# Splitting an early input transfer, moving a small one to another queue, and setting products further from the transfers that feed them, in a one-core attention and feed-forward kernel

## The chip, the core and the metric

The kernel runs on one core of one Trainium2 chip. The metric is the device time of one execution in microseconds (us). Each kernel was executed five or six times in a set of runs, beside the kernel before on the same chip. A profile belongs to one of those executions; its span is 1.73 us shorter than the device time of the same execution (155.57 less 153.84 before).

## The reference, cut to what matters

```python
# x: 2048 tokens x 448; wqkv 448 x 1344; w_phi 16 x 28 x 28; wo 448 x 448; w1 448 x 1792; w2 1792 x 448; bf16
xn = layernorm(x)
q, k, v = heads(xn @ wqkv)                       # 16 heads of 28
phi(t) = concat(softmax(t @ w_phi), softmax(-(t @ w_phi)))
o = (phi(q) @ (phi(k).T @ v)) / (phi(q) @ sum(phi(k)) + 1e-6)     # linear attention
out = x + o @ wo + silu(xn @ w1) @ w2
```

## The kernel before

The kernel has a list of operations with dependencies, and a greedy scheduler that orders them per engine when the program is built, from modelled durations. `chain` adds order alone. `cur_slack` makes the scheduler place a product that much later than the modelled end of what it waits for; it is not a wait on the chip.

The loads are issued in this order (SP queue unless `eng` says otherwise):

```python
load(Wp[:], A_w_phi.rearrange("(g hl) d f -> (hl d) g f", g=G), "wphi", eng="act", lat=3000.0)
load_x(0, 1)
load_x(1, 2)
load_x(2, 4)                     # token tiles 2 and 3 in one transfer
load_w1(0, 512, 3200.0)          # two transfers each: 384 rows, and the last 128
load_w1(512, 1024, 3200.0)
load_x(4, 8)
load_w1(1024, FF)
# ... wv, x tiles 8 to 15, w2, wo
```

`w_phi` is 448 pieces of 56 bytes. The layernorm of tiles 0 to 3 goes through DVE and ACT, and PE transposes them; tiles 4 to 15 go through DVE and POOL, and a transposing DMA takes two tiles at a time:

```python
def ln_tile(t):                  # cut
    # bn_stats, bn_aggr (DVE); sqrt on ACT and reciprocal, or pow on POOL; (x - mean) * rstd (DVE)
    if t >= XN_DMA0:             # 4
        if t % 2:
            dma_t(xnT[:, t - 1:t + 1, :, :]..., xn_sb[:, sl - 1:sl + 1, :]..., 1300.0, f"xnT_dma{t}")
        return
    transposes(...)              # tiles 0 to 3, on PE
```

At the start PE computes 38 products of ones that nobody reads, to bring its clock up. Then come the transposes of tiles 0 and 1, then ffn1 (w1) for tiles 0 to 3. The next products that need new tokens are those of ffn1 for tiles 4 to 7, which I call the second quarter:

```python
for i in range(38):
    P.op("pe", 107.0, ... banks[3][:, 0:128], ones_bf[:], ones_bf[:] ..., name="warm")
# ...
for t in range(4):
    ln_tile(t)
fold()                           # block diagonal of w_phi, one POOL operation
chain("ev0 ve2 ev1 ve3 ev2 silu_table".split())
# ... ffn1 of tiles 0 to 3: F(0) to F(6); v of tiles 0, 1
for n, t in ((7, 2), (10, 4)):   # F(7) is the first product that needs tiles 4 to 7
    group([F(n, 0), v_block(t, AUX)], [F(n + 1, 2), F(n + 2, 4)], "rem")
```

The output stage multiplies by wo what a transposing DMA delivers:

```python
def wo_fulls(q, ob, cs, st):
    P.cur_slack = 900.0
    for n in range(3):
        mm(ob, oT_sb[:, q, n + q % 2, :], wo_sb[:, q % 2, n, cs], st and n == 0, False, "wo_mm")
    P.cur_slack = 0.0
```

The softmax here doesn't subtract the row's maximum and nothing guards it: scores larger than these inputs give would overflow.

## Time and profile before

| | us |
|---|---|
| median of the first three executions | 153.57 (153.53 to 153.88) |
| the profiled execution | 155.57, span 153.84 |
| PE busy | 148.2 |

From the page of the kernel before: the span, PE's busy time with its number of instructions, then PE's busy tenths and the granted PE clock in tenths, in 40 equal slices of the span.

```profile
span 153.8 us, 2800 instructions
...
PE 148.2 (96%) x1118; PEld 79.4 (52%) x1118; DVE 90.0 (59%) x171; ACT 72.6 (47%) x86; POOL 67.4 (44%) x76
...
PE   7599999999999999999999999999999999999993
...
PEclk9959999999999999999999999999999999999999
```

PE is the limit; only the head is loose, and the clock was down in the third slice. From the table of waits of the kernel before, PE alone (us in total, times, longest):

```profile
PE psum L438 <- DMA phT<-in_B_w_dram: 1.3, 1, 1.3
PE psum L490 <- POOL ones_bf L465: 1.1, 1, 1.1
PE psum L453 <- DVE rstd L569: 0.4, 1, 0.4
PE psum L438 <- DMA vaug<-vaug: 0.2, 1, 0.2
```

`phT<-in_B_w_dram` is w1 (it borrows that tile's room), and `vaug<-vaug` is a transposing DMA ahead of wo.

The stretches of the head (bounds and length, then for PE, PE's weight loads, DVE, ACT and POOL the busy time and count, then clock, DMA share, GB/s), for the kernel before:

```profile
4.00:6.00 2.00, 1.56 (x21) 1.19 (x18) 1.56 (x6) 0.86 (x3) 0.30 (x1) 1.00 0.93 302
6.00:7.45 1.45, 0.12 (x3) 0.03 (x1) 1.12 (x3) 0.60 (x3) 0.00 (x0) 1.00 1.05 356
7.45:9.40 1.95, 1.95 (x22) 1.95 (x23) 1.29 (x6) 0.75 (x3) 0.00 (x0) 0.58 1.04 382
9.40:10.90 1.50, 1.50 (x17) 1.50 (x16) 0.00 (x0) 1.04 (x2) 0.00 (x0) 0.50 1.06 390
```

### The profile page before, as it was taken

How to read it: one execution, taken by the hardware profiler on the slowest of the kernel's cores; microseconds unless marked ns; L12 is line 12 of the kernel's file. 1: busy time of each engine (PE TensorE's matmuls, PEld its weight loads, DVE VectorE, ACT ScalarE, POOL GpSimd, SP SyncE). 2: the span in 40 equal slices, each digit the busy share in tenths (PEclk: the TensorE clock that was granted, in tenths of full speed). 3: DMA queues.
4: the chain of work that ended last, by engine and by line, in shares of the span. 5: the costliest groups of instructions: out<-in, count | busy, mean ns of one | idle time of the engine just before them, and what ended most of it. 6: DMA issues, size and time to landing. Idle time of an engine off the chain costs nothing.

```text
span 153.8 us, 2800 instructions
## 1 busy us (share of the span) xinstructions
PE 148.2 (96%) x1118; PEld 79.4 (52%) x1118; DVE 90.0 (59%) x171; ACT 72.6 (47%) x86; POOL 67.4 (44%) x76
## 2 busy tenths in 40 slices
PE   7599999999999999999999999999999999999993
PEld 7497444446444556545434444445554455555482
DVE  1748888306019998897112521999973724474552
ACT  3452884676688669698555759784000000000000
POOL 7105564300014999999993000499997000000000
PEclk9959999999999999999999999999999999999999
DMA  5997554799940000000058311065899993144151
GB/s 90 320 387 285 112 105 81 91 240 280 238 137 0 4 0 0 9 0 0 4 114 161 66 34 38 0 122 98 171 124 191 207 199 68 39 124 124 36 155 64
DMA packets 44206, 17.38 MB, mean 113 GB/s; under 512 B 36640, under 2 KB 43808, under 8 KB 44192
## 3 DMA queue, kind: packets, MB, share of 16 engines
q1 hardware_dynamic: 41568, 15.44, 45.3%
q10 hardware_dynamic: 2624, 1.75, 3.8%
q8 instruction: 9, 0.15, 0.4%
q14 instruction: 5, 0.04, 0.1%
HBM read 6.56 MB, written 1.84 MB: 55 GB/s over the span
## 4 chain that ended last, share of the span: by engine, by line
PE 91%; DMA 6%; SPq 1%; issue 0%; DVE 0%
PE psum L438 90%; DMA phT<-in_B_w_dram 3%; DMA vaug<-vaug 3%; SPq L499 1%; PE psum L453 1%; DVE x_sb L776 0%
## 5 line engine op out<-in xcount | busy, mean ns | idle before, releaser
L438 PE MATMUL psum<-xnT,phT 128*128 128x512 bf16 (+2 forms) x278 | 49.2, 346 | 1.3 <-DMA phT<-in_B_w_dram 1.3
L438 PE MATMUL psum<-w_sb,hT 128*128 128x448 bf16 (+1 forms) x238 | 48.6, 342 | 0.0
L458 ACT ACTIVATE hT<-psum 128x1024 bf16<-128x1024 f32 x28 | 27.9, 1025 | 18.8 <-PE psum L438 18.8
L706 POOL TENSOR_TENSOR RA<-Ek_sb,Rec 128x896 bf16<-128x896 bf16 x16 | 26.6, 1700 | 16.3 <-DVE Rec L674 16.3
L438 PEld LDWEIGHTS psum<-xnT,phT 128*128 128x128 bf16 (+1 forms) x278 | 21.1, 102 | 21.6 <-issue 4.7
L438 PEld LDWEIGHTS psum<-w_sb,hT 128*128 128x128 bf16 x238 | 22.2, 98 | 17.4 <-issue 0.6
L673 DVE TENSOR_REDUCE Rec<-Ek_sb 128x64 f32<-128x1792 bf16 x12 | 23.7, 1978 | 12.0 <-ACT Ek_sb L458 12.0
L458 ACT ACTIVATE Ek_sb<-psum 128x896 bf16<-128x896 f32 x24 | 20.4, 927 | 5.0 <-PE psum L438 2.3
L681 POOL TENSOR_TENSOR Ek_sb<-Ek_sb,Rec 128x896 bf16<-128x896 bf16 x8 | 13.3, 1698 | 5.7 <-DVE Rec L674 5.6
L753 DVE TENSOR_SCALAR den<-psum 128x16 f32<-128x16 f32 x16 | 2.7, 171 | 19.6 <-PE psum L438 19.6
L438 PE MATMUL psum<-wv,xnT 128*128 128x448 bf16 (+1 forms) x64 | 13.5, 352 | 0.0
L438 PE MATMUL psum<-Wk,xnT 128*128 128x448 bf16 (+1 forms) x64 | 13.5, 353 | 0.0
L681 POOL TENSOR_TENSOR phT<-phT,Rec 128x896 bf16<-128x896 bf16 x8 | 13.3, 1706 | 0.0
L438 PE MATMUL psum<-Wq,xnT 128*128 128x448 bf16 (+1 forms) x64 | 12.5, 353 | 0.0
L438 PE MATMUL psum<-wo_sb,vaug 128*128 128x448 bf16 (+1 forms) x51 | 11.7, 342 | 0.2 <-DMA vaug<-vaug 0.2
L563 DVE BATCH_NORM_STATS2 st<-x_sb 128x6 f32<-128x448 bf16 x16 | 9.6, 602 | 3.7 <-DMA x_sb<-in_A_x_dram 3.7
L776 DVE TENSOR_TENSOR x_sb<-psum,x_sb 128x448 bf16<-128x448 f32 (+1 forms) x13 | 7.1, 583 | 5.9 <-PE psum L438 5.8
L760 DVE TENSOR_TENSOR vaug<-psum,rden 128x448 bf16<-128x448 f32 x16 | 10.0, 624 | 0.8 <-DVE rden L755 0.2
L578 DVE TENSOR_SCALAR RA<-x_sb,mv,rstd 128x384 bf16<-128x384 bf16 (+2 forms) x28 | 8.8, 350 | 2.7 <-POOL rstd L574 2.6
L674 DVE RECIPROCAL Rec<-Rec 128x64 f32<-128x64 f32 x16 | 8.7, 546 | 0.3
L673 DVE TENSOR_REDUCE Rec<-phT 128x64 f32<-128x1792 bf16 x4 | 8.0, 1990 | 0.9 <-ACT phT L458 0.9
L572 POOL TENSOR_SCALAR ve<-mv 128x1 f32<-128x1 f32 x12 | 2.6, 217 | 13.2 <-DVE mv L564 13.2
(49 smaller groups left out, 118.2 us busy)
## 6 DMA issues: line engine op xcount, KB each, us to landing
out_dram<-x_sb ACTq DMA_DIRECT2D x15, 112.0 KB, 2.6
w_sb<-in_B_w_dram SPq DMA_DIRECT2D x1, 1568.0 KB, 8.0
x_sb<-in_A_x_dram SPq DMA_DIRECT2D x3, 448.0 KB, 7.4
phT<-in_B_w_dram SPq DMA_DIRECT2D x2, 384.0 KB, 5.3
wo_sb<-in_A_wo_dram SPq DMA_DIRECT2D x2, 336.0 KB, 4.0
phT<-in_B_w_dram SPq DMA_DIRECT2D x1, 576.0 KB, 7.1
wv<-in_A_wqkv_dram SPq DMA_DIRECT2D x1, 336.0 KB, 7.2
phT<-in_B_w_dram SPq DMA_DIRECT2D x2, 128.0 KB, 5.2
```

The source lines that it names most:

```text
L438: r = e.matmul(dst, lhsT, rhs, start=st, stop=sp, skip_group_check=True)
L458: P.op("act", d_act(n), lambda e: e.activation(dst, src, func, scale=scale), reads=[src], writes=[dst], table=table, name=name, **keys)
L563: P.op("dve", 590, lambda e: e.bn_stats(st6[:, t, :], xs), reads=[xs], writes=[st6[:, t, :]], name=f"bnst{t}", okeys_w=["ln"])
L572: P.op("pool", 200, lambda e: e.tensor_scalar(ve[:, t:t + 1], mv[:, t, 1:2], EPS_LN, None, ALU.add), reads=[mv[:, t, 1:2]], writes=[ve[:, ...
L578: P.op("dve", dur, lambda e: e.tensor_scalar(dst, x_sb[:, t, c0:c1], mv[:, t, 0:1], rstd[:, t:t + 1], ALU.subtract, ALU.mult), reads=[xs, ...
L673: P.op("dve", 1985, lambda e: e.tensor_reduce(R2, E4, AXL.X, ALU.add), reads=[E4], writes=[R2], name="Ssum")
L674: P.op("dve", 555, lambda e: e.reciprocal(R2, R2), reads=[R2], writes=[R2], name="Rrec")
L681: P.op("pool", 1700, lambda e: e.tensor_tensor(E3, E3, Rk[:, :, None].broadcast_to([128, 32, DH]), ALU.mult), reads=[E3, Rk], writes=[E3], ...
L706: P.op("pool", 1700, lambda e: e.tensor_tensor(dst, Eq, Rq.rearrange("p (c j) -> p c j", c=CC)[:, :, :, None].broadcast_to([128, CC, 4, DH ...
L753: P.op("dve", 190, lambda e: e.tensor_scalar(den[:, uq, :], U3[:, :, DH], EPS_DEN, None, ALU.add), reads=[U3[:, :, DH]], writes=[den[:, uq ...
L760: P.op("dve", 620, lambda e: e.tensor_tensor(o3, U3[:, :, 0:DH], rden[:, uq, :, None].broadcast_to([128, H, DH]), ALU.mult), reads=[U3[:, ...
L776: P.op("dve", d_dve(cs.stop - cs.start), lambda e: e.tensor_tensor(res[:, cs], ob, addend[:, cs], ALU.add), reads=[ob, addend[:, cs]], wri ...
```

## The change

Its intent: let the first tiles and w1 come sooner, by taking w_phi's small pieces out of the head and letting tile 2 arrive without tile 3; and take away the last wait of a wo product.

```diff
-        load(Wp[:], A_w_phi.rearrange("(g hl) d f -> (hl d) g f", g=G), "wphi", eng="act", lat=3000.0)
         load_x(0, 1)
         load_x(1, 2)
-        load_x(2, 4)
+        load_x(2, 3)
+        load_x(3, 4)
         load_w1(0, 512, 3200.0)
@@ wo_fulls, and the same in finish_tile
-            P.cur_slack = 900.0
+            P.cur_slack = 1500.0
@@
-        fold()
         act(warm_act[:], ones_bf[:, 0:4], ACTF.Silu, 4, "silu_table", table="silu", okeys_w=["sq"])
-        chain("ev0 ve2 ev1 ve3 ev2 silu_table".split())
+        load(Wp[:], A_w_phi.rearrange("(g hl) d f -> (hl d) g f", g=G), "wphi", eng="act", lat=3000.0)
+        chain("ev0 ve2 ev1 ve3 ev2 silu_table wphi".split())
@@ after the layernorm of tiles 4 to 7
         chain("ev3 bnst4".split())
+        fold()
+        chain("rstd7 bdphi".split())
```

w_phi was on the scalar queue already; it is now issued there later. The order of operations on PE changes only around the transposes of tiles 2 and 3 and around the wo products.

More of the change, by code (lines that the diff above doesn't have):

```diff
@@ L790, in finish_tile @@
                 wo_fulls(q, ob, cs, t < NYT)
-                P.cur_slack = 900.0
+                P.cur_slack = 1500.0
                 pe_mms([wo_rem(q, ob, slice(0, 128), cs)], "wo_mm")
```

## The prediction

> **What bounds it.** The matrix engine (PE): busy 148.2 of 153.8 us (first table), 91% of the chain of waits. Its waits (table of waits): 1.3 us for w1's first transfer, 1.1 us for the ones tile at the start, 0.4 us for the first layernorm, 0.2 us for one transposing DMA before a wo product at 123.2 us. Only the head, that gap and the PE clock can give anything. The table of stretches shows clock 0.58 from 7.45 to 9.40 us and 0.50 to 10.90 us; 128-column matmuls start 107 ns apart there, 56 ns later. [...] (half from 7.76 to 11.17 us). It costs 1.7 us.
>
> **The head in the trace.** x tiles 0 and 1 land at 3.1 and 3.5 us, tiles 2 and 3 (one transfer) at 6.27, w1's first block at 7.32, issued at 2.20. Between 2.9 and 5.4 us most of the 16 DMA engines hold one packet of tiles 2 and 3 for 0.4 to 1.4 us; others of that size take 74 ns. They come just behind w_phi's 448 packets of 56 B. [...] I take the stall to be w_phi's, unproved.
>
> **What the change does.**
> - Takes w_phi out of the head. If the stall goes, w1's first block lands near 5.7 us (estimate: issue 0.45 us later, first packet 1.1 us after issue, 24 packets per engine at 47 ns, 0.4 us to land). Then the copy of transposed tile 0 gates PE (ends at 6.33 us): PE starts near 6.4, not 7.45 us: 1.0 us.
> - ACT's second copy, queued behind a square root of tile 2, ends near 7.3, not 7.96 us.
> - One more issue on the SP queue: w1 and later loads are issued 0.45 us later, the loss if the stall stays.
> - w_phi's issue (0.42 us on ACT) falls in a 2.8 us hole; its product (0.93 us on POOL) in a 1.48 us hole after rstd 7. Free.
> - wo products move behind more ffn2 matmuls of 0.19 us: removes the 0.2 us wait, adds no work (1118 matmuls as before).
>
> **Clock.** With PE back at 6.4 us, the window from 4.35 to 7.76 us holds about twice the matmul work. If that keeps the clock full, 1.7 us more come, less what later loads take back.
>
> **Sum.** Stall gone, half-clock stays: 1.0 + 0.2, 152.4 us (35%). Stall and half-clock gone: 2.2 + 0.2, 151.2 us (25%). Stall stays: 0 to 0.3, 153.4 us (40%). Predicted **152.4 us**, 151.0 to 153.7 us 8 times in 10. Faster by over 2% 0.07, within 2% 0.92, slower 0.01.
>
> **What shows it.** Right: PE's wait for w1 under 0.5 us; no 1 us packets in tiles 2 and 3; w1's first block lands before 6.3 us; no wait at 123 us; PE busy the same, or 1.5 us less if the clock row has no 5. Wrong: w1 lands at 7.3 us or later.
>
> **What would make it wrong.** The slow packets come from something else; the stall moves with w_phi to 12 us and delays x tiles 4 to 7 or w1's last block; a late w_phi blocks POOL and the layernorm of tiles 8 and 9.

The sum: 1.0 (PE's start) and 0.2 us (the wo wait) off 153.6 us, 152.4 us. So was the paragraph on the clock, behind the 151.2 us branch: in the trace of before PE was busy for 1.66 us from 4.34 to 7.76 us and the clock was 0.50 in the next 3.41 us, but that the second follows from the first is not shown. The estimate of 5.7 us is from the same trace: one issue on the SP queue takes 0.45 us, tile 0's first packet started 1.04 us after its issue, w1's 1 KB packets took 46 ns in the median and 49 in the mean, and w_phi landed 0.44 us after its last packet. Its terms, counted from w1's issue at 2.20 us, come to 5.3 us.

## More of the kernel before

From the timeline of the kernel before (start, duration, engine, line, operation, count, and in brackets the idle time before it with what ended it):

```profile
6.30 0.63 DVE L563 BATCH_NORM_STATS2 st<-x_sb 128x6 f32<-128x448 bf16 x1 [0.63 <-DMA x_sb<-in_A_x_dram]
...
7.45 1.93 PE L438 MATMUL psum<-xnT,phT 128*128 128x128 bf16 x19 [1.33 <-DMA phT<-in_B_w_dram]
...
11.25 0.62 DVE L563 BATCH_NORM_STATS2 st<-x_sb 128x6 f32<-128x448 bf16 x1
...
20.68 2.75 PE L438 MATMUL psum<-xnT,phT 128*128 128x512 bf16 x12
```

The first line is tile 2's statistics, the second the first ffn1 products, the third tile 4's statistics, which wait for nothing here. The last is six products of tiles 0 to 3 and then the first six of the second quarter, without a pause.

## The result, and the profile after

| | before | after |
|---|---|---|
| median of five executions, us | 153.56 (153.33 to 153.88) | 153.48 (153.14 to 153.89) |
| ratio | | 0.9993, 95% interval 0.997 to 1.0016 |
| profiled execution, us | 155.57 | 153.50 |
| span, us | 153.84 | 151.77 |

Ratios here and below are the mean time of one kernel's fast runs over that of the other's of the same rounds, so they are not quite the ratio of the medians quoted. By the 2% rule of the verdicts every run below is "the same" as the kernel before; what is said of smaller differences rests on the intervals and on the traces.

The medians say: the same. The two profiles differ by 2.07 us. Both are true, because the profile of before belongs to an execution that took 2.0 us more than that kernel's median. From the page after, the lines shown of before:

```profile
span 151.8 us, 2800 instructions
...
PE 147.0 (97%) x1118; PEld 78.3 (52%) x1118; DVE 90.5 (60%) x171; ACT 72.5 (48%) x86; POOL 67.4 (44%) x76
...
PE   7799999999999999999999999999999999999993
...
PEclk9999999999999999999999999999999999999999
```

PE's waits in the kernel after, whole:

```profile
PE psum L490 <- POOL ones_bf L465: 1.1, 1, 1.1
PE psum L438 <- ACT xnT L458: 0.9, 1, 0.9
```

The second line is again the wait for w1: the first transfer of its first block landed at 6.98 us and the product began at 7.11, while the copy of transposed tile 0 had ended at 6.38 us; the profile names what it saw last. The timeline after:

```profile
5.43 0.62 DVE L563 BATCH_NORM_STATS2 st<-x_sb 128x6 f32<-128x448 bf16 x1
...
7.11 1.22 PE L438 MATMUL psum<-xnT,phT 128*128 128x128 bf16 x19 [0.93 <-ACT xnT L458]
...
10.94 0.63 DVE L563 BATCH_NORM_STATS2 st<-x_sb 128x6 f32<-128x448 bf16 x1 [1.42 <-DMA x_sb<-in_A_x_dram]
...
18.72 2.94 PE L438 MATMUL psum<-xnT,phT 128*128 128x512 bf16 x12
```

Three things are to be seen. Tile 2's statistics start 0.87 us sooner, as intended. The first 19 products take 1.22 us where they took 1.93: the clock. And tile 4's statistics, which used to wait for nothing, now wait 1.42 us for x tiles 4 to 7; the twelve products across the border to the second quarter take 2.94 us where they took 2.75, so PE waited 0.2 us inside them. The stretches after:

```profile
4.00:6.00 2.00, 2.00 (x21) 1.71 (x18) 1.89 (x7) 0.72 (x3) 0.00 (x0) 1.00 0.83 234
6.00:7.45 1.45, 0.52 (x9) 0.37 (x8) 1.34 (x7) 1.33 (x4) 0.00 (x0) 1.00 1.08 364
7.45:9.40 1.95, 1.95 (x38) 1.95 (x36) 0.80 (x4) 0.79 (x2) 0.00 (x0) 1.00 1.00 335
9.40:10.90 1.50, 1.50 (x30) 1.50 (x28) 0.12 (x1) 1.30 (x2) 0.00 (x0) 1.00 1.05 370
```

### The profile page after: what moved, and what is told of

It is laid out like the page before. It is cut to its first block, busy times and chain, and to the rows that moved or that the text cites. A ratio compares the mean times of both kernels' runs of the same rounds, so it can differ in the third digit from the quotient of the medians.

```text
span 151.8 us, 2800 instructions
## 1 busy us (share of the span) xinstructions
PE 147.0 (97%) x1118; PEld 78.3 (52%) x1118; DVE 90.5 (60%) x171; ACT 72.5 (48%) x86; POOL 67.4 (44%) x76
## 5 line engine op out<-in xcount | busy, mean ns | idle before, releaser
L438 PE MATMUL psum<-xnT,phT 128*128 128x512 bf16 (+2 forms) x278 | 48.1, 338 | 1.0 <-ACT xnT L458 0.9
L438 PEld LDWEIGHTS psum<-xnT,phT 128*128 128x128 bf16 (+1 forms) x278 | 19.8, 97 | 21.6 <-issue 3.2
L458 ACT ACTIVATE Ek_sb<-psum 128x896 bf16<-128x896 f32 x24 | 20.4, 927 | 5.0 <-PE psum L438 2.3
L438 PE MATMUL psum<-wo_sb,vaug 128*128 128x448 bf16 (+1 forms) x51 | 11.4, 341 | 0.0
L578 DVE TENSOR_SCALAR RA<-x_sb,mv,rstd 128x384 bf16<-128x384 bf16 (+2 forms) x28 | 9.3, 367 | 2.9 <-POOL rstd L574 2.7
```

What stands on the lines that cost most here:

```text
L438: r = e.matmul(dst, lhsT, rhs, start=st, stop=sp, skip_group_check=True)
L458: P.op("act", d_act(n), lambda e: e.activation(dst, src, func, scale=scale), reads=[src], writes=[dst], table=table, name=name, **keys)
L578: P.op("dve", dur, lambda e: e.tensor_scalar(dst, x_sb[:, t, c0:c1], mv[:, t, 0:1], rstd[:, t:t + 1], ALU.subtract, ALU.mult), reads=[xs, ...
```

## The experiments

Two questions: what was the 2 us between the profiles, and why did nothing of the change reach the median? Theory A: the clock of the head is a lottery from one execution to the next, and the profile of before drew a bad ticket. Theory B: the change removed the half-clock window (7.76 to 11.17 us in the profile of before, products 107 ns apart) and lost 2 us elsewhere. Theory C, for the second question: PE's path and the path of x tiles 4 to 7 meet at the first product of the second quarter, near 20 us; the change shortens nothing on the first, and the split lengthens the second. Its rival: only PE's own path counts.

All runs, each kernel in six executions beside eleven or twelve of the kernel before on the same chip (sets 3 and 4 on one chip; the twelve of set 4 are the eleven of set 3 and one more, so these two sets are not independent of each other):

| set, median of before | kernel | median (range), us | ratio, 95% interval |
|---|---|---|---|
| 1, 153.59 | b_again | 153.60 (152.91 to 155.03) | 1.0009, 0.9966 to 1.0052 |
| | p_phi | 153.54 (153.12 to 153.87) | 0.9992, 0.9960 to 1.0024 |
| | p_split | 153.79 (153.45 to 154.06) | 1.0008, 0.9978 to 1.0038 |
| | p_slack | 153.08 (152.89 to 153.41) | 0.9964, 0.9932 to 0.9997 |
| 2, 153.82 | n_split | 153.13 (152.47 to 154.46) | 0.9940, 0.9884 to 0.9996 |
| | f_before | 154.14 (153.87 to 154.81) | 1.0007, 0.9958 to 1.0055 |
| | f_after | 153.75 (153.59 to 153.94) | 0.9979, 0.9932 to 1.0026 |
| | x4_early | 153.30 (152.96 to 153.48) | 0.9947, 0.9895 to 0.9999 |
| 3, 153.52 | after_2 | 153.73 (152.66 to 154.87) | 1.0020, 0.9974 to 1.0065 |
| | n_split_2 | 152.78 (152.53 to 152.98) | 0.9954, 0.9929 to 0.9979 |
| | x4_late | 155.01 (154.66 to 156.63, and 304.21; 154.95 without that one) | 1.0109, 1.0066 to 1.0151 |
| | warm16 | 155.34 (154.77 to 155.97) | 1.0117, 1.0087 to 1.0147 |
| 4, 153.53 | x4_late_2 | 154.94 (154.36 to 155.65) | 1.0092, 1.0060 to 1.0124 |
| | n_phi | 153.41 (153.00 to 154.76) | 1.0005, 0.9970 to 1.0041 |
| | n_slack | 153.86 (153.60 to 155.16) | 1.0034, 1.0000 to 1.0068 |
| | n_split_3 | 152.87 (152.57 to 153.10) | 0.9956, 0.9932 to 0.9980 |

Read from the traces, one execution each (us): when the first transfer of w1's first block (384 of its rows) and x tiles 4 to 7 had landed, how much more the first 70 real products took than 70 times 56 ns, when the first product of the second quarter began, and from there to the end of the span.

| kernel | w_phi, tiles 2 and 3 | w1 lands | x 4 to 7 land | extra, 70 products | second quarter begins | to the end |
|---|---|---|---|---|---|---|
| before | early, joined | 7.32 | 10.20 | 1.61 | 21.98 | 131.86 |
| b_again | early, joined | 6.98 | 10.52 | 1.50 | 21.53 | 131.78 |
| p_slack | early, joined | 6.49 | 10.07 | 0.27 | 19.92 | 131.47 |
| p_phi | late, joined | 5.87 | 9.59 | 0 | 19.57 | 131.82 |
| n_split | late, joined | 6.63 | 10.06 | 0 | 20.06 | 131.47 |
| n_split_2 | late, joined | 5.93 | 9.27 | 0.15 | 19.32 | 131.48 |
| n_split_3 | late, joined | 5.90 | 9.43 | 0 | 19.37 | 131.48 |
| p_split | early, split | 6.58 | 10.96 | 0 | 20.78 | 131.55 |
| n_phi | early, split | 6.51 | 10.88 | 0.46 | 20.60 | 131.54 |
| after | late, split | 6.98 | 10.92 | 0 | 20.21 | 131.56 |
| after_2 | late, split | 6.66 | 10.96 | 0 | 20.82 | 131.56 |
| n_slack | late, split | 7.14 | 11.12 | 0.38 | 20.80 | 131.56 |

The last column is nearly constant. Whatever these kernels gain or lose, they do ahead of the second quarter, except for 0.3 us in the tail. Two kernels outside the table, with the old slack and joined tiles, lost more in the tail: f_before took 132.08 and warm16 132.41 us to the end, and their PE waits there for the transposing DMA were 0.3 and 0.4 us.

### The kernel before again (b_again)

No edit.

> The kernel before, unchanged, to see its usual execution. Device time less span was 1.73 us in both profiles (155.57 - 153.84 and 153.50 - 151.77), so theory A (the profile of before caught one rare execution with a half-clock window, and the median never had it) expects spans of 151.6 to 152.1 us and a granted clock of 1.00 in at least 4 of 5 executions, and a profile with no 5 in the clock row and w1's first block landing near 7.0 us. Rival B (before has the half-clock window as a rule, and the change removed it but lost 2 us outside the span) expects a clock of 0.99 and spans of 153.6 to 154.0 us.

Five of the six spans were 151.2 to 152.3 us, a little wider than the 151.6 to 152.1 of theory A and far from the 153.6 to 154.0 of theory B, which has fallen. The sixth, again the one that was profiled, took 155.03 us. Its page shows no 5 in the clock row, so that part of the expectation missed, but its products say otherwise. Timeline of b_again:

```profile
7.12 2.19 PE L438 MATMUL psum<-xnT,phT 128*128 128x128 bf16 x19 [0.77 <-DMA phT<-in_B_w_dram]
9.10 0.63 PE L453 MATMUL psum<-ident,RA 128*128 128x128 bf16 x4
```

19 products in 2.19 us, against 1.22 at full clock: 107 ns apart. The 38 warming products are that far apart to the last one, so here the clock had not risen before 10.3 us, where in before it rose at 4.34 and fell again at 7.76. The clock's record of that execution begins only at 10.32 us, and the page takes what came before as full. The spacing of equal matmuls is the better witness. It is not the profiler that makes an execution slow: the profiled executions of n_split_2, n_split_3 and f_before were the fastest of their six, and three unprofiled ones of before took 155.09 to 155.32 us in set 2.

### One part of the change alone (p_phi, p_split, p_slack)

```diff
 p_phi:    before, with w_phi loaded late and its product after rstd 7
 p_split:  before, with  -load_x(2, 4)  +load_x(2, 3)  +load_x(3, 4)
 p_slack:  before, with  -P.cur_slack = 900.0  +P.cur_slack = 1500.0  (twice)
```

> Only w_phi late on the scalar queue. If w_phi's small writes were the stall of the head: w1's first block lands 0.5 us or more earlier than in b_again, 0.3 us or more faster. If the stall has another cause: w1's landing and the time the same within 0.15 us.

The time is that of before (153.54 against 153.59), though w1 landed at 5.87 us, over 1 us sooner than in b_again. The head ran ahead and then met x tiles 4 to 7: the transposing DMA of tiles 6 and 7 landed at 19.44 us and the product that needs it began at 19.57. The first branch of the expectation was right about w1 and wrong about the time.

> Only tiles 2 and 3 in two transfers. One more issue of 0.45 us ahead of w1. If w1's landing is set by the issue: 0.3 to 0.45 us slower. If it is set by the DMA engines' backlog: the same within 0.15 us.

153.79 us, not clearly slower. w1 was not late; x tiles 4 to 7 were, at 10.96 us, and PE then waited 1.0 us for the transposing DMA of their layernorm. Neither branch of the expectation had named that path.

> Only the larger slack of the wo products. Expected the same within 0.2 us, at most 0.2 us faster, as the one wait that it can remove was 0.22 us; no PE wait on a transposing DMA of oT in the profile.

0.5 us below before in the median, more than the 0.2 us expected. The tail accounts for 0.3 of it (131.47 against 131.78 to 131.86 us to the end), and the wait is gone. The rest lies within the spread of the heads. The head of this kernel is that of before, so its trace (153.12 us) is also the best view of a usual one: the first 19 products took 1.26 us, and the first 70 products were 56 ns apart but for one stop of 0.19 us: no half clock.

### The split undone in the changed kernel (n_split, n_split_2, n_split_3)

```diff
-        load_x(2, 3)
-        load_x(3, 4)
+        load_x(2, 4)
```

> The changed kernel with tiles 2 and 3 in one transfer again. Theory C (two paths meet at the first products of the second quarter of tokens, near 20 us: PE's own path, and the landing of x tiles 4 to 7 plus about 9.8 us through layernorm and two transposing DMAs; the split's extra issue delays the second path) expects x tiles 4 to 7 to land at 9.6 to 10.2 us instead of 10.9 and 0.2 to 0.5 us less time than the changed kernel: median 153.0 to 153.3 us. If the split is harmless or helps, 153.4 us or more.

> The changed kernel with tiles 2 and 3 in one transfer, again. Theory C: 0.2 to 0.5 us less than after_2 in the median of the executions, x tiles 4 to 7 landing at 9.6 to 10.2 us. If n_split's 153.13 us was chance: equal to after_2 within 0.15 us.

> The changed kernel without the split, a third time, as the base of these four. Median 152.7 to 153.2 us, 0.4 to 0.9 us less than the kernel before and less than n_phi and n_slack.

In three sets of runs this kernel was faster than the kernel before, in the last two by 0.74 and 0.66 us of the medians, and on that chip 0.95 and 0.86 us below the changed kernel, after_2; more than theory C had said at first (0.2 to 0.5 us below the changed kernel). after_2's six executions spread widely (152.66 to 154.87), and one of them lies among those of n_split_2. x tiles 4 to 7 landed at 9.27 to 10.06 us instead of 10.92 and 10.96. It beats both kernels: the one before by 0.45% (0.9954 and 0.9956), and after_2 by 0.6% of the medians. The two other kernels of set 4 that keep the split, n_phi and n_slack, lie above it as well (153.41 and 153.86). PE's waits in n_split_3:

```profile
PE psum L490 <- POOL ones_bf L465: 1.1, 1, 1.1
PE psum L438 <- ACT xnT L458: 0.6, 1, 0.6
```

and in after_2, the changed kernel in an execution of 154.10 us:

```profile
PE psum L490 <- POOL ones_bf L465: 1.1, 1, 1.1
PE psum L438 <- DMA xnT<-RA: 1.0, 1, 1.0
PE psum L438 <- DMA phT<-in_B_w_dram: 0.8, 1, 0.8
```

`xnT<-RA` is the transposing DMA of tiles 4 to 7. The timeline of after_2 shows where it ends up:

```profile
10.99 0.63 DVE L563 BATCH_NORM_STATS2 st<-x_sb 128x6 f32<-128x448 bf16 x1 [1.78 <-DMA x_sb<-in_A_x_dram]
...
20.82 1.46 PE L438 MATMUL psum<-xnT,phT 128*128 128x512 bf16 x6 [0.95 <-DMA xnT<-RA]
```

DVE waits 1.78 us for x tiles 4 to 7, and 9.83 us later PE waits for what came of them.

### The changed kernel again (after_2)

No edit.

> The changed kernel again, beside n_split_2 and the kernel before on one chip. Theory C (the split costs what the late w_phi and the larger slack gain) expects a median within 0.3 us of the kernel before, x tiles 4 to 7 landing at 10.4 to 11.0 us, first product of the second quarter of tokens at about 20.2 us.

0.21 us above before in the median, no clear difference, with a wide range. x tiles 4 to 7 landed just as expected; the second quarter began at 20.82 us, 0.6 later than expected and than in the first profile.

### Longer and shorter ways for x tiles 4 to 7 (x4_late, x4_late_2, x4_early)

```diff
 n_split, and in x4_late, x4_late_2:
-        load_x(4, 8)
         load_w1(1024, FF)
+        load_x(4, 8)
 n_split, and in x4_early:
+        load_x(4, 8)
         load_w1(512, 1024, 3200.0)
-        load_x(4, 8)
```

> n_split with x tiles 4 to 7 loaded behind w1's last block, so the suspected path is made longer and everything ahead of it on PE is left alone. Theory C: they land near 11.7 instead of 10.1 us, the first product of the second quarter comes near 21.5 us (about 9.8 us later, 4 v products of 0.19 us slip in before it), PE waits about 1 us there on the transposing DMA, and the median is 0.6 to 1.2 us above n_split_2. If only PE's own path counts: within 0.2 us of n_split_2.

Its profile can't be read: that execution took 304.21 us (span 302.5, of which PE waited 1.4), so PE ran at half pace, at a granted clock recorded as 1.00. Four of the other five, 154.66 to 155.07 us, were about 2.1 us above n_split_2, more than expected (the fifth took 156.63). So it was run again.

> x tiles 4 to 7 behind w1's last block, again[...]. Theory C: they land near 11.8 us, the wait of PE on the transposing DMA before the first product of the second quarter is 1 us or more, that product comes about 9.8 us after the layernorm of tile 4 begins, and the median is 1.5 to 2.3 us above n_split_3 (x4_late's usual executions were at 154.66 to 155.07). Against theory C: the product comes later than PE's own path by less than 0.3 us, and the time is lost elsewhere.

2.07 us above n_split_3. x tiles 4 to 7 landed at 11.78 us. Timeline of x4_late_2:

```profile
11.80 0.63 DVE L562 BATCH_NORM_STATS2 st<-x_sb 128x6 f32<-128x448 bf16 x1 [2.69 <-DMA x_sb<-in_A_x_dram]
...
22.46 1.02 PE L438 MATMUL psum<-xnT,phT 128*128 128x512 bf16 x4 [1.45 <-DMA xnT<-RA]
```

PE's first ffn1 products began at 6.26 us here, among the earliest of all, and that did nothing for the time: the second quarter waited. It came 10.66 us after tile 4's statistics, not 9.8; the second transposing DMA was issued 3.27 us after the first, where it is 2.54 in n_split_3. That is most of why the loss was larger than first expected. The edit had also changed the scheduler's order: DVE takes tile 8's statistics (at 16.04 us) ahead of the last normalising of tiles 6 and 7, and PE four products of v ahead of the second quarter. PE's own path was only 0.24 us longer than in n_split_3 up to the first 512-column product (12.23 against 11.99 us), and the two spans differ by 2.34. So the rival of theory C has fallen.

> n_split with x tiles 4 to 7 loaded ahead of w1's second block. Theory C expects them to land near 8 us, no wait of PE on the transposing DMA near 20 us, and 0.2 to 0.8 us less than n_split, unless w1's second block, now near 9.5 us, stops PE earlier. If PE's own path alone counts: the same or slower.

No wait near 20 us, as expected, and tile 4's statistics at 9.09 us. But 153.30 us is not less than n_split: the first 70 products took 0.61 us more. Of this, 0.35 is a stop for ACT's copy of transposed tile 2 (it ended at 8.84 us, the product began at 8.89), not for w1's second block, which landed at 9.12; n_split has no such stop. This part missed: with this load order PE's own path was the longer one.

### The clock of the head (f_before, f_after, warm16)

```diff
 f_before, f_after: after the transpose of tile 1, ahead of the first ffn1 product
+        for i in range(10):
+            P.op("pe", 107.0, ... ones_bf, ones_bf ..., name=f"fill{i}")
 warm16: before, with
-        for i in range(38):
+        for i in range(16):
```

> The kernel before with 10 more products of ones between the second transpose and the first ffn1 product, where PE waits anyway[...]. If the 2 us spread of the executions of before (152.87 to 155.03) is the half-clock window: no execution above 153.9 us, spread below 0.8 us, matmuls at 56 ns from 8 us on. If the spread has another cause, such as the landing of w1: spread as before, above 1.5 us over as many executions.

By its numbers it missed: all but one execution lay above 153.9 us and the range was 0.94 us, not below 0.8. In the trace the products were 56 ns apart from 8 us on, as expected. No execution reached 155 us, while three of the eleven of the kernel before in the same set did (155.09, 155.25, 155.32); but in sets 1, 3 and 4 none of before did either, so six executions don't show that the fillers take the slow ones away. The median rose to 154.14 us; in the trace the loss is in the tail (132.08 us to the end, against 131.78 to 131.86), and its cause was not followed up.

> The changed kernel with the same filler. If the changed kernel's head is faster, it must show here[...]: 0.5 us or more faster than f_before. Theory C expects only the wo part, 0.3 us, less what the split costs: 0.3 us faster to 0.2 us slower than f_before.

0.39 us below f_before, a little more than theory C's range. By the traces it is all tail (131.55 against 132.08 us to the end); the second quarter begins later than in f_before, at 20.41 against 20.06 us. No 0.5 us came from the head.

> The kernel before with 16 warming products of ones instead of 38. If activity[...] sets the clock of the head: the clock is half in nearly every execution until 9 to 11 us, the first 70 real products take 1.3 to 1.7 us more than at full clock, and the median is 1.0 to 2.0 us above the kernel before. If the slow executions of before come from the landing of w1: the median stays within 0.3 us of it.

1.82 us above before, as expected, and the first 70 products took 1.99 us more than at full clock (1.3 to 1.7 expected). Timeline of warm16:

```profile
6.92 2.19 PE L438 MATMUL psum<-xnT,phT 128*128 128x128 bf16 x19 [0.57 <-DMA phT<-in_B_w_dram]
```

w1 was not late here (6.78 us), the clock was low; 0.5 to 0.6 us more of this execution's loss is in the tail (132.41 us to the end). Three traces of this case show an extra of 1.5 us or more in the first 70 products at usual load order: before (155.57 us), b_again (155.03) and warm16 (155.97).

### The other two parts undone (n_phi, n_slack)

```diff
 n_phi:    the changed kernel, with w_phi's load first again and fold() back in its place
 n_slack:  the changed kernel, with cur_slack 900 again
```

> The changed kernel with w_phi early again (split and slack kept). If the late w_phi is worth 0.1 to 0.3 us in the changed kernel: median 153.6 to 153.9 us if that of before is near 153.55. If it is worth nothing: as the changed kernel, 153.5.

153.41 us, 0.32 below after_2, with ranges that overlap: the late w_phi gives the changed kernel nothing that shows.

> The changed kernel with the old slack (late w_phi and split kept). From the profiles the stretch after the second half of the q blocks takes 46.05 us with the old slack and 45.70 with the new: 0.2 to 0.4 us slower than the changed kernel, 153.7 to 154.1 us, the slowest of the three.

153.86 us against 153.73, so the slack gives the changed kernel nothing that shows either. The reason is in the table: to the end it is 131.56 us with the old slack and with the new. With the split, the wait ahead of wo is gone already (p_split, 131.55, shows the same). The expectation's 0.2 to 0.4 us missed for that.

## Why the prediction was wrong

The time, 153.48 us, lies inside the range; the gain of 1.2 us that the number was built on (1.0 from an earlier start of PE, 0.2 from the wo wait, taken off 153.6) is not there. The sum's likeliest single branch, "Stall stays: 0 to 0.3, 153.4 us (40%)", has nearly the measured time, but not for its reasons: it looked for the loss at w1's landing and did not see x tiles 4 to 7. That is in part luck. Of the prediction's own tests, the wait at 123 us is gone, but w1 landed at 6.98 us, neither before 6.3 nor after 7.3, and PE's wait for it was 0.9 us, not under 0.5. Point by point:

- **"Its waits ... 1.3 us for w1's first transfer" and "half from 7.76 to 11.17 us ... It costs 1.7 us".** Read rightly, from the wrong execution. The profiled one took 155.57 us, the median was 153.57, and both were known. Subtracting the excess of device time over span shows that the usual span was 151.8 us already. The half-clock window (1.61 us in the first 70 products) was not in the usual execution, so no change could remove it there (the 19 products of p_slack, with the same head, took 1.26 us). This is the first step that failed: it carries the branch of 1.7 us, and the 7.45 us that the next step starts from. Nor does the slow stretch keep one place: the clock's record has boundaries at 4.34, 7.76 and 11.17 us in before, and begins at 6.57 in after and at 5.29 in n_split. In before and after all its stretches but the last, which the trace's end cuts, are whole multiples of 3.41 us (1, 1 and 42 in before, 43 in after).
- **"PE starts near 6.4, not 7.45 us: 1.0 us."** This step carried the number, and it failed. PE started at 7.11 and 6.80 us in the two profiles of the changed kernel and at 7.28 in n_slack, which has its head; with an early w_phi and joined tiles at 7.45, 7.12, 6.62, 7.10 and 6.92 us (before, b_again, p_slack, f_before, warm16). So nothing of the 1.0 us is there. The late w_phi alone does bring w1 sooner: with joined tiles it landed at 5.87 to 6.63 us instead of 6.49 to 7.32. The split takes that back (6.66 to 7.14 us with both).
- **"I take the stall to be w_phi's."** In part. With tiles 2 and 3 joined, their packets, summed over the 16 engines, took 8.0 to 11.4 us more than their usual time (74 ns a packet in before) with w_phi early (five traces) and 4.1 to 7.0 us with w_phi late (six), and the tiles landed at 5.47 to 6.27 us against 4.52 to 5.57. But other long packets stayed: of all packets of the first tiles and of w1 up to 7 us, the excess was 13.4 to 15.9 us with w_phi early and 11.5 to 17.1 with w_phi late; in the changed kernel it was 15.0. What causes the rest stays open.
- **"w1 and later loads are issued 0.45 us later, the loss if the stall stays."** The size of the issue was right (w1 was issued at 2.67 instead of 2.20 us), the place of the loss was missed. It is not w1, it is x tiles 4 to 7: 10.9 us instead of 10.2. Their layernorm and two transposing DMAs take 9.3 to 10.0 us from tile 4's statistics to the first product of the second quarter in the nine traces where PE waits for them at the usual load order (10.7 in x4_late_2). In these traces the product begins 0.13 to 0.14 us after the second transposing DMA has landed. The prediction named these tiles only under what would make it wrong, delayed by a stall that moves with w_phi; it had no second path in its sum. This is the second step that failed: a gain ahead of 20 us cannot pass that meeting point unless both paths get shorter. x4_late_2 (2.07 us for 2.35 us of later landing than n_split_3) shows it from the one side, n_split_2 and n_split_3 from the other. The delay of x tiles 4 to 7 is larger than the 0.47 us of the issue. Part of it shows between 4 and 5 us: with w_phi late and the tiles split, the DMA engines moved only 107 to 149 GB/s there (after, after_2, n_slack, f_after; DMA share 0.62 to 0.74), with w_phi late and the tiles joined 279 to 342 (six traces), with w_phi early 205 to 299 (seven). So the lower rate came only with the two parts together; its cause is not shown.
- **"removes the 0.2 us wait"** Right for the wait; it was 0.3 us. But the split alone removes it too (p_split), so the slack was needed only without the split.
- **"Free" for w_phi's later issue and product.** No loss shows.

The sum, as measured in the traces and the medians: the tail gives 0.3 us; the head loses 0.2 to 0.4 us. (The usual span of before, 151.8 us, less 131.8 to the end, puts the start of the second quarter at 20.0 us; the changed kernel's two medians, 153.48 and 153.73, less 1.73 and 131.56, put it at 20.2 and 20.4.) Together: the same. This split of the sum is worked out from medians and single traces, and its parts are no larger than the spread of the executions.

## What to carry to other kernels

Before reading a gain out of a profile, check that its execution is a usual one: its device time against the median, and equal matmuls against their spacing at full clock (here 56 ns, and 107 in the slow stretches). Where two paths meet, follow the second one to its first wait before counting what the first can save: here one more transfer issued ahead of a later load cost as much as the rest of the change gave (0.95 us from n_split_2 to after_2, against 0.74 from before to n_split_2). And try each part alone and each part undone; the parts did not add up here, and the best kernel left one of them out.

## What stays open

- How much warming-up the clock takes. What it lacked made 1.5 to 2.0 us of 154 us in three traces (1.61 in before, 1.50 in b_again, 1.99 in warm16), more than any part of the change, and decided which profile one was looking at. 38 products of ones followed by 8 transposes were followed by full clock in some executions (p_slack, 0.27 us extra) and not in others (before, b_again), and 16 products gave 1.99 us extra.
- The clock's record can begin late and be read as full clock before: b_again, whose record begins at 10.32 us, and warm16 show 1.00 while products started 107 ns apart.
- What one more issue costs the loads behind it. In this head an issue takes about 0.45 us on the SP queue (three in 1.36 us before, four in 1.83 after), and one more of them came with a landing of x tiles 4 to 7 that was later by about 0.7 us with w_phi early (means of 10.26 and 10.92) and by 1.4 with it late (9.59 and 11.00).
- The cause of the long packets. I blamed w_phi's 56-byte pieces for packets of 0.4 to 1.4 us. Those of tiles 2 and 3 shrank when w_phi had moved, but others stayed (up to 0.9 us in after, 1.7 us in n_split).
- With one more transfer on the SP queue near the start, the transposing DMA ahead of the wo product that waited (the eighth of `vaug`) landed 40.0 to 40.3 us after the first product with `KVm` (six traces), where it landed after 41.6 to 42.1 us in the kernels with joined tiles (eleven traces). The cause is open.
- A whole execution with PE at half pace: one of x4_late took 304.21 us, the five others 154.66 to 156.63.
